# Queries and keys of the first batch entry loaded three rows to a partition and turned by paired products

## The chip, the cores and the metric

One core of one Trainium2 chip runs the whole program. Its engines work side by side, each through its own list of instructions in order: TensorE (PE, with its weight loads shown as PEld), VectorE (DVE), ScalarE (ACT), GpSimd (POOL), and SyncE (SP), which issues the transfers between HBM and on-chip memory. The metric is the device time of one execution in microseconds, the median of several runs.

## What is computed

Attention, then a mixture of eight experts, then a dense layer, all in float32. Two batch entries, eight heads, 576 positions, 64 columns a head:

```python
q_d = q.reshape(B, H, Sd, factor, D).mean(axis=3)      # factor 4, Sd = 144; k_d, v_d alike
out_up = np.repeat(sm_attn(q_d, k_d, v_d), factor, axis=2)
mask = np.abs(pos[:, None] - pos[None, :]) < factor
scores = np.where(mask, scale * q @ k.T, -1e9)
out_local = softmax(scores) @ v
x = (out_up + out_local)                               # then 1152 x 512
...
for e in range(E):
    out += P[:, e:e + 1] * (np.maximum(x @ w1[e], 0.0) @ w2[e])
...
g = softplus(x @ w_in); return g @ w_out
```

So each head has a local part (each position sees those less than four away) and a grouped part (means of four rows attend to means of four rows, and the result is repeated four times).

## The kernel before

The attention runs in eight units of two heads each: units 0 to 3 are batch entry 0, units 4 to 7 entry 1. The stream of work takes the units in order, and of each unit four blocks: "c", the grouped part, and 0, 1, 2, thirds of the 576 positions. For a block, `scores` puts scores into a bank and makes the softmax (maxima on DVE, three exponentials on ACT, sums and scaling on DVE), `turn` transposes the result on PE, and `values` multiplies it with the values. `turn` lags two blocks and `values` three. For units 0 to 3 each `scores` and nearly each `turn` also issues a `stir`, a 128x512 bf16 product of the identity that nobody reads.

Before that, `load_qk` fetches a unit's queries and keys in four transfers (queries and keys, two heads). Partition p holds row 64t + p of the queries (p below 64) or of the keys (64 above), for nine tiles t, the two heads side by side: pieces of 64 floats, 256 B. `setup(g)` is called for three groups of three tiles. It turns each tile with one `nc.tensor.transpose` of 128x128 (L534) into the bank `tb`; DVE adds fours of columns into `qkd` (L539, the grouped queries and keys); ACT scales the keys into `kT` (L550); DVE and ACT copy the two heads' queries into the halves of `fine[g]` (L551, L552), three buffers that all units share. With the third group DVE scales the grouped queries into `flat` (L545). With the first, POOL adds the grouped values `vd` into `vs` (L559, L560).

`load_v` fetches the value windows `vw` (L516, L520; two buffers) and `vd` (L523; one buffer, `bufs=1`, for all units, so that each load waits until POOL has added the one before). Units 0 and 3 take one buffer `qk` for queries and keys; units 1 and 2 borrow places of the first layer's weights, `w1h` and `w1l`, not needed yet.

SP's list is in program order as the scheduler placed it, and a transfer at its head that has to wait holds up all behind it. The expert weights come in through it too (L263, L308); ACT and POOL split them into a high and a low part. From the middle of the attention, pieces of the first expert's products (L866, L954) stand between the attention's products on PE. What is issued where is set by a scheduler, which orders each engine's list by its own estimate; from the second expert on, a planner in the kernel sets it.

Of the kernel before, what the change touches and what calls it, by code (L numbers as in the profile page):

```python
# [9 lines left out]
F32 = mybir.dt.float32  # L10
F32R = mybir.dt.float32r
# [3 lines left out]
ALU = mybir.AluOpType  # L15
AX = mybir.AxisListType
# [4 lines left out]
def attention_moe_mlp(ctx: ExitStack, tc: tile.TileContext, q, k, v, w_gate, w1, w2, w_in, w_out, out):  # L21
    nc = tc.nc
    B, H, S, D = q.shape
    NT, DM = out.shape
    E, _, FF = w1.shape
    F2 = w_out.shape[0]
    P = 128
    R = 4
    SD = S // R
    HC = SD // 2  # L30
    QT = 64
    NQ = S // QT
    NB = 3
    CT = SD // NB
    KW = QT + 2 * R
    KD = DM // P
    SCALE = 1.0 / float(D) ** 0.5
# [19 lines left out]
    wp = ctx.enter_context(tc.tile_pool(name="wp", bufs=3))  # L57
# [4 lines left out]
    rows = [ctx.enter_context(tc.tile_pool(name="rows0", bufs=len(TILES[0])))]  # L62
# [32 lines left out]
    ident = const.tile([P, P], F32, name="ident")  # L95
# [357 lines left out]
    ap = at.__enter__()  # L453
# [18 lines left out]
    fine = [ap.tile([P, NB, 2, QT], F32, bufs=1, name=f"fine{g}") for g in range(NB)]  # L472
# [11 lines left out]
    class Unit:  # L484
# [12 lines left out]
        def load_qk(self):  # L497
            b, h0 = self.b, 2 * self.u
            if self.n in (1, 2):
                qk = wp.tile([P, OPS, 2, P], F32R, tag="w1h" if self.n == 1 else "w1l", name="qkw").bitcast(F32)  # L500
                qk = qk.rearrange("p a k c -> p (a k c)")[:, : NQ * 2 * D]
                qk = qk.rearrange("p (t h d) -> p t h d", t=NQ, h=2)
            else:
                qk = ap.tile([P, NQ, 2, D], F32, tag="qk", bufs=1, name="qk")
            self.qk = qk
            for w, src in enumerate((q, k)):
                for hh in range(2):
                    nc.sync.dma_start(
                        qk[w * QT : (w + 1) * QT, :, hh], src[b, h0 + hh].rearrange("(t p) d -> p t d", p=QT)
                    )  # L510

        def load_v(self):
            b, h0 = self.b, 2 * self.u
            self.vw = vw = ap.tile([KW, NQ, 2, D], F32, tag="vw", name="vw")
            for t, w0 in ((0, 0), (NQ - 1, S - KW)):
                nc.sync.dma_start(vw[:, t], v[b, h0 : h0 + 2, w0 : w0 + KW, :].rearrange("h p d -> p h d"))  # L516
            for hh in range(2):
                src = v[b, h0 + hh, QT - R :, :]
                windows = bass.AP(tensor=src.tensor, offset=src.offset, ap=[[D, KW], [QT * D, NQ - 2], [1, D]])
                nc.sync.dma_start(vw[:, 1 : NQ - 1, hh], windows)  # L520
            self.vd = vd = ap.tile([HC, 2, 2, R, D], F32, tag="vd", bufs=1, name="vd")
            for hh in range(2):
                nc.sync.dma_start(vd[:, :, hh], v[b, h0 + hh].rearrange("(c p r) d -> p c r d", c=2, r=R))  # L523

        def setup(self, g):

            if g == 0:
                self.kT = ap.tile([P, NQ, QT], F32, tag="kT", name="kT")
                self.qkd = ap.tile([P, NQ, 2, QT // R], F32, tag="qkd", name="qkd")
            qkd = self.qkd  # L530
            tb = self.bank("tb", 1)
            tiles = slice(NB * g, NB * g + NB)
            for j in range(NB):
                nc.tensor.transpose(  # L534
                    tb[:, j * P : (j + 1) * P], self.qk[:, NB * g + j].rearrange("p h d -> p (h d)"), ident
                )
            tb = tb[:, : NB * P]
            tbv = tb.rearrange("x (t w p) -> x t w p", t=NB, w=2)
            nc.vector.tensor_reduce(  # L539
                qkd[:, tiles].rearrange("x t w g -> x (t w) g"),  # L540
                tb.rearrange("x (t g r) -> x t g r", g=QT // R, r=R), axis=AX.X, op=ALU.add,
            )
            for hh in range(2 if g == NB - 1 else 0):
                half = slice(hh * D, (hh + 1) * D)
                nc.vector.tensor_scalar(  # L545
                    self.flat[half, :, hh].rearrange("x i (j g) -> x i j g", j=NB),
                    qkd[half, :, 0].rearrange("x (i j) g -> x i j g", i=NB),
                    SCALE / (R * R), None, op0=ALU.mult,
                )
            nc.scalar.mul(self.kT[:, tiles], tbv[:, :, 1], SCALE)  # L550
            nc.vector.tensor_copy(fine[g][:D, :, 0], tbv[:D, :, 0])  # L551
            nc.scalar.copy(fine[g][D:, :, 1], tbv[D:, :, 0])  # L552
            if g:
                return
            vd = self.vd

            self.vs = vs = ap.tile([HC, 2, 2, D], F32, tag="vs", name="vs")
            for c in range(2):
                nc.gpsimd.tensor_tensor(vd[:, c, :, 0:2, :], vd[:, c, :, 0:2, :], vd[:, c, :, 2:4, :], op=ALU.add)  # L559
                nc.gpsimd.tensor_tensor(vs[:, c], vd[:, c, :, 0, :], vd[:, c, :, 1, :], op=ALU.add)  # L560
# [505 lines left out]
    for n in range(len(stream) + LAG + 1):  # L1066
        if n < len(stream):
            x, blk = stream[n]
            i, j = divmod(n, len(blocks))
# [49 lines left out]
    half, short, done = logits()  # L1119
# [46 lines left out]
    with tc.manual_schedule(engines=engines):  # L1166
# [74 lines left out]
```

## Time and profile before

| | |
|---|---|
| median of 3 runs | 1068.11 us (1066.86 to 1068.22) |
| profiled execution | 1065.88 us, span 1064.0 us |
| PE busy | 1044.2 us, 98% of the span |
| DVE, ACT, POOL busy | 692.5, 570.0, 556.1 us |
| DMA packets under 512 B | 36000 of 135799 |
| mean granted TensorE clock | 0.995 |

The span runs from the first to the last instruction of the program; the execution's own time is 1.88 us longer. An engine's busy time is taken from its instructions' records, and those of PE overlap, so the distance from the start of one group to the start of the next tells better what a product costs. A clock of 1.00 is 2.4 GHz, of 0.50 is 1.2 GHz.

### The profile page before, as it was taken

Reading aid. Unit: us, or ns where it says so; the run is one execution under the profiler, and the core shown is the slowest. Engines: PE = TensorE matmul, PEld = TensorE weight load, DVE = VectorE, ACT = ScalarE, POOL = GpSimd, SP = SyncE. Lnnn points to the kernel's source line nnn. Section 1 sums busy time; section 2 is a strip of 40 time slices with the busy share of each in tenths; the row PEclk is TensorE's granted clock in tenths of the full one; section 3 lists DMA queues with packets and bytes.
Section 4 is the critical chain, followed back from the end, with each engine's and each line's share of the span. In section 5 each row is a group of like instructions: output and inputs, shape, how many; then the busy total and the mean of one; then the engine's idle time right before and its main releaser. Section 6 shows DMA issues by size and latency. Waiting matters only on the chain.

```text
span 1064.0 us, 17733 instructions
## 1 busy us (share of the span) xinstructions
PE 1044.2 (98%) x6417; PEld 925.7 (87%) x6417; DVE 692.5 (65%) x1416; ACT 570.0 (54%) x1479; POOL 556.1 (52%) x575
## 2 busy tenths in 40 slices
PE   7989999999999999999999999999999999999998
PEld 5778888898999989898998989899998999888897
DVE  4896666765656566566756665665664677876674
ACT  4887654435444444454444445444544667666664
POOL 3658433487556575555556666664574413222322
PEclk8999999999999999999999999999999999999999
DMA  9463201233333335243333333443334485533752
GB/s 175 131 136 84 85 21 41 61 94 114 95 115 90 99 94 154 80 128 114 117 114 94 101 108 94 118 126 100 119 99 140 147 295 211 217 149 129 262 202 80
DMA packets 135799, 131.22 MB, mean 123 GB/s; under 512 B 36000, under 2 KB 112032, under 8 KB 135712
## 3 DMA queue, kind: packets, MB, share of 16 engines
q1 hardware_dynamic: 135712, 130.10, 39.9%
q8 instruction: 50, 0.82, 0.3%
q14 instruction: 37, 0.30, 0.1%
HBM read 104.64 MB, written 25.43 MB: 122 GB/s over the span
## 4 chain that ended last, share of the span: by engine, by line
PE 83%; DVE 8%; ACT 5%; POOL 2%; DMA 1%; issue 1%; SPq 0%; ACTq 0%
PE yps L954 41%; PE m L866 37%; POOL ab L830 2%; DVE ab L833 1%; ACT one L828 1%; DVE ab L826 1%; PE sc L582 1%; DVE one L824 1%; DVE xl L439 1%; DVE c L885 1%; PE pv L641 1%; DMA raw<-in_moe_w 1%; ACT ab L815 1%; PE tp L619 1%; PE sc L569 1%
## 5 line engine op out<-in xcount | busy, mean ns | idle before, releaser
L866 PE MATMUL m<-xh,w1h 128*128 128x320 f32 (+1 forms) x1120 | 333.8, 298 | 3.5 <-ACT t L878 2.4
L866 PE MATMUL m<-xl,w1h 128*128 128x320 f32 (+1 forms) x1120 | 331.7, 296 | 1.1 <-DVE xl L439 1.1
L866 PE MATMUL m<-xh,w1l 128*128 128x320 f32 (+1 forms) x1120 | 331.6, 296 | 0.0
L866 PEld LDWEIGHTS m<-xh,w1h 128*128 128x128 f32 x1120 | 211.8, 189 | 20.1 <-ACT t L878 4.0
L866 PEld LDWEIGHTS m<-xl,w1h 128*128 128x128 f32 x1120 | 211.9, 189 | 14.4 <-DVE xl L439 1.5
L866 PEld LDWEIGHTS m<-xh,w1l 128*128 128x128 f32 x1120 | 211.8, 189 | 0.3 <-issue 0.2
L954 PE MATMUL yps<-w2h,hh 128*128 128x512 f32 x502 | 198.9, 396 | 0.0
L954 PE MATMUL yps<-w2l,hh 128*128 128x512 f32 x502 | 198.3, 395 | 0.0
L954 PE MATMUL yps<-w2h,hl 128*128 128x512 f32 x502 | 195.9, 390 | 0.0
L954 PE MATMUL yps<-w2h,h 128*128 128x512 f32 x436 | 152.8, 392 | 0.0
L293 POOL TENSOR_TENSOR w1l<-sums,w1h 128x512 fp32r<-128x512 f32 x72 | 99.5, 1394 | 90.9 <-ACT w1h L291 79.3
L885 DVE TENSOR_TENSOR c<-m,t 128x256 f32<-128x256 f32 (+1 forms) x160 | 72.8, 455 | 114.0 <-PE m L866 68.8
L314 POOL TENSOR_TENSOR w2l<-raw,w2h 128x512 fp32r<-128x512 f32 x72 | 98.8, 1391 | 60.0 <-ACT w2h L312 59.8
L803 ACT ACTIVATE hh<-c 128x256 fp32r<-128x256 f32 (+1 forms) x138 | 60.8, 444 | 127.7 <-DVE c L885 127.5
L830 POOL TENSOR_TENSOR ab<-one,ab 128x320 f32<-128x320 f32 (+1 forms) x64 | 55.3, 866 | 141.0 <-ACT one L828 140.9
L984 DVE SCALAR_TENSOR_TENSOR acc<-yps,pr,acc 128x512 f32<-128x512 f32 x117 | 87.2, 745 | 53.0 <-PE yps L954 52.4
L805 DVE SCALAR_TENSOR_TENSOR hl<-c,hh 128x256 fp32r<-128x256 f32 (+1 forms) x138 | 93.3, 679 | 31.7 <-ACT hh L803 30.1
L954 PEld LDWEIGHTS yps<-w2h,hl 128*128 128x128 f32 x502 | 94.4, 188 | 21.6 <-issue 0.2
L954 PEld LDWEIGHTS yps<-w2h,hh 128*128 128x128 f32 x502 | 94.7, 189 | 12.5 <-DVE small L589 0.2
L878 ACT COPY t<-m 128x256 f32<-128x256 f32 (+1 forms) x160 | 62.6, 398 | 77.9 <-PE m L866 77.7
L954 PEld LDWEIGHTS yps<-w2l,hh 128*128 128x128 f32 x502 | 94.8, 189 | 10.7
L954 PEld LDWEIGHTS yps<-w2h,h 128*128 128x128 f32 x436 | 82.1, 188 | 14.7
(141 smaller groups left out, 1647.2 us busy)
## 6 DMA issues: line engine op xcount, KB each, us to landing
raw<-in_moe_w SPq DMA_DIRECT2D x72, 256.0 KB
raw<-in_moe_w SPq DMA_DIRECT2D x36, 512.0 KB
w1h<-s_in SPq DMA_DIRECT2D x14, 896.0 KB
w1l<-s_in SPq DMA_DIRECT2D x14, 896.0 KB
raw<-in_moe_w_in SPq DMA_DIRECT2D x32, 256.0 KB
raw<-in_moe_w_out SPq DMA_DIRECT2D x16, 512.0 KB
w2l<-s_out SPq DMA_DIRECT2D x14, 512.0 KB
w2h<-s_out SPq DMA_DIRECT2D x14, 512.0 KB
```

Source lines behind the costliest of these rows:

```text
L293: behind(chain, nc.gpsimd.tensor_tensor(lo[:, part], sums, hi[:, part].bitcast(F32), op=ALU.subtract))
L314: behind(chain, nc.gpsimd.tensor_tensor(lo[:, i], raw[:, i], hi[:, i].bitcast(F32), op=ALU.subtract))
L439: nc.vector.tensor_tensor(xl[s][:, i, kk], src, xh[s][:, i, kk].bitcast(F32), op=ALU.subtract)
L569: nc.tensor.matmul(sc[:rows, i * w : (i + 1) * w], self.flat[:, i].rearrange("x h q -> x (h q)"), self.qkd[:, :, 1], start=True, stop=True,)
L803: nc.scalar.activation(hh, c, AF.Relu)
L805: nc.vector.scalar_tensor_tensor(out=hl, in0=c, scalar=0.0, in1=hh.bitcast(F32), op0=ALU.max, op1=ALU.subtract)
L830: nc.gpsimd.tensor_tensor(ab, one, ab, op=ALU.subtract)
L866: nc.tensor.matmul(b[:, :h], x[:, i, kk, :], y[s][:, i, kk, :], start=(not more and n == 0), stop=(n == 5), skip_group_check=more,)
L878: nc.scalar.copy(t, b[:, :h])
L885: nc.vector.tensor_tensor(c, b[:, :h], t, op=ALU.add)
L954: nc.tensor.matmul(y, a[:, f, tok], b[:, f, :], start=(start and m == 0), stop=(stop and m == 5))
L984: nc.vector.scalar_tensor_tensor(out=acc[t], in0=y, scalar=pr[:, t, e : e + 1], in1=acc[t], op0=ALU.mult, op1=ALU.add,)
```

## The change

For units 0 to 3, `load_qk` reads the rows as (g p j): partition p of group g holds rows 192g + 3p + j, j from 0 to 2, which lie one behind the other in memory, so a piece is 192 floats, 768 B. In the buffer the head now stands outside of j, and a turned tile would mix heads; so each transpose becomes two products with the identity, one for each head (64 stationary columns), which write 64 partitions of the bank, every third column. The bank then holds queries and keys in the order of the positions. The bank's order is changed for all units (queries ahead of keys); units 4 to 7 keep loads and transposes. The grouped values of units 1 and 2 go into places of the second layer's weights, `w2h` and `w2l`.

```diff
             if self.n in (1, 2):
                 qk = wp.tile([P, OPS, 2, P], F32R, tag="w1h" if self.n == 1 else "w1l", name="qkw").bitcast(F32)
                 qk = qk.rearrange("p a k c -> p (a k c)")[:, : NQ * 2 * D]
+            else:
+                qk = ap.tile([P, NQ * 2 * D], F32, tag="qk", bufs=1, name="qk")
+            self.thirds = self.n < 4
+            if self.thirds:
+                qk = qk.rearrange("p (g h j d) -> p g h j d", g=NB, h=2, j=NB)
+            else:
                 qk = qk.rearrange("p (t h d) -> p t h d", t=NQ, h=2)
-            else:
-                qk = ap.tile([P, NQ, 2, D], F32, tag="qk", bufs=1, name="qk")
...
+                    rows = src[b, h0 + hh]
+                    if self.thirds:
+                        rows = rows.rearrange("(g p j) d -> p g j d", g=NB, j=NB)
+                    else:
+                        rows = rows.rearrange("(t p) d -> p t d", p=QT)
+                    nc.sync.dma_start(qk[w * QT : (w + 1) * QT, :, hh], rows)
...
-            self.vd = vd = ap.tile([HC, 2, 2, R, D], F32, tag="vd", bufs=1, name="vd")
+            if self.n in (1, 2):
+                vd = wp.tile([P, 2, DM], F32R, tag="w2h" if self.n == 1 else "w2l", name="vdw").bitcast(F32)
+                vd = vd[:HC].rearrange("p a (h r d) -> p a h r d", h=2, r=R)
+            else:
+                vd = ap.tile([HC, 2, 2, R, D], F32, tag="vd", bufs=1, name="vd")
...
             for j in range(NB):
-                nc.tensor.transpose(
-                    tb[:, j * P : (j + 1) * P], self.qk[:, NB * g + j].rearrange("p h d -> p (h d)"), ident
-                )
+                if self.thirds:
+                    to = tb.rearrange("x (w p j) -> x w p j", w=2, j=NB)[:, :, :, j]
+                    for hh in range(2):
+                        nc.tensor.matmul(
+                            to[hh * D : (hh + 1) * D], self.qk[:, g, hh, j],
+                            ident.rearrange("k (w p) -> k w p", w=2), start=True, stop=True,
+                        )
+                else:
+                    to = tb.rearrange("x (w t p) -> x w t p", w=2, t=NB)[:, :, j]
+                    nc.tensor.transpose(to, self.qk[:, NB * g + j].rearrange("p h d -> p (h d)"), ident)
```

The scheduler's order shifts with it. DVE near the start, where units 0 and 1 are set up and the first softmax begins (`small` holds the maxima; `fine_147` to `fine_149` are the three groups' queries, `flat_150` and `flat_151` the grouped queries of units 0 and 1), before:

```order
L539 TENSOR_REDUCE qkd<-tb 128x96
L551 COPY fine_149<-tb 64x3x64
L551 COPY fine_147<-tb 64x3x64
L539 TENSOR_REDUCE qkd<-tb 128x96
L551 COPY fine_148<-tb 64x3x64
L589 TENSOR_REDUCE small<-sc 96x3
L589 TENSOR_REDUCE small<-sc 128x3 x2
L539 TENSOR_REDUCE qkd<-tb 128x96
L545 TENSOR_SCALAR flat_151<-qkd 64x3x48 x2
L595 TENSOR_SCALAR small<-sc 96x3
```

and with the change:

```order
L557 TENSOR_REDUCE qkd<-tb 128x96
L568 COPY fine_149<-tb 64x3x64
L568 COPY fine_147<-tb 64x3x64
L557 TENSOR_REDUCE qkd<-tb 128x96
L606 TENSOR_REDUCE small<-sc 96x3
L606 TENSOR_REDUCE small<-sc 128x3 x2
L568 COPY fine_148<-tb 64x3x64
L557 TENSOR_REDUCE qkd<-tb 128x96
L563 TENSOR_SCALAR flat_151<-qkd 64x3x48 x2
L612 TENSOR_SCALAR small<-sc 96x3
```

The three reductions for the maxima moved ahead of the copy into `fine_148`.

PE in the middle of entry 0, where unit 3 is turned (`tb`) beside unit 2's scores (`sc`) and unit 1's values (`pv`), before:

```order
L582 MATMUL sc<-kT,fine_147 128x72 x3
L534 MATMUL tb<-ident,qk 128x128 x6
L630 MATMUL pv<-etc,vs 64x144 x4
L619 MATMUL tp<-ident,ex 72x128 x3
L479 LDWEIGHTS identb
L479 MATMUL sc<-identb 128x512
L576 LDWEIGHTS identb
L576 MATMUL sc<-mask,identb 128x216
L582 MATMUL sc<-kT,fine_148 128x72 x3
```

and with the change:

```order
L586 MATMUL sc<-qkd,flat_150 96x144 x3
L550 MATMUL tb<-ident,qk 64x128 x3
L647 MATMUL pv<-etc,vs 64x144 x4
L636 MATMUL tp<-ident,ex 72x128 x3
L479 LDWEIGHTS identb
L479 MATMUL sc<-identb 128x512
L593 LDWEIGHTS identb
L593 MATMUL sc<-mask,identb 128x216
L599 MATMUL sc<-kT,fine_148 128x72 x3
L550 MATMUL tb<-ident,qk 64x128 x9
```

Of twelve products that stand for six transposes, three stay ahead of the values and the rest went behind the scores of `fine_148`, with three of the next group; the last six of unit 3 stand behind a block's values. Unit 2's eighteen stand as 7, 5 and 6, each group between other work.

SP, from unit 2's queries and keys to the first expert's weights (`raw_584`, `raw_694`) and the value windows, before:

```order
L508 DMA qkw<-in_q 64x9x64 x2
L508 DMA qkw<-in_k 64x9x64 x2
L508 DMA qk<-in_q 64x9x64
L523 DMA vd<-in_v 72x2x256 x2
L508 DMA qk<-in_q 64x9x64
L508 DMA qk<-in_k 64x9x64 x2
L685 DMA wg<-in_moe_w_gate 128x4x8
L263 DMA raw_584<-in_moe_w 128x4x128 x2
L308 DMA raw_694<-in_moe_w 128x2x512
L523 DMA vd<-in_v 72x2x256 x4
L516 DMA vw<-in_v 72x2x64 x2
```

and with the change (`vdw` are the borrowed places):

```order
L535 DMA vdw<-in_v 72x2x256 x2
L517 DMA qkw<-in_q 64x3x192 x2
L517 DMA qkw<-in_k 64x3x192 x2
L535 DMA vdw<-in_v 72x2x256 x2
L517 DMA qk<-in_q 64x3x192 x2
L517 DMA qk<-in_k 64x3x192 x2
L702 DMA wg<-in_moe_w_gate 128x4x8
L535 DMA vd<-in_v 72x2x256 x2
L263 DMA raw_611<-in_moe_w 128x4x128 x2
L308 DMA raw_727<-in_moe_w 128x2x512
L523 DMA vw<-in_v 72x2x64 x2
```

The grouped values of units 1 to 3 moved ahead of the first expert's weights, and only unit 3's still takes the shared buffer.

## Rows read from the trace of the kernel before

**Rows 1.** Windows: stretch, its length, busy PE, PEld, DVE, ACT, POOL, PEclk, DMA share, GB/s

```profile
13.60:16.70 3.10, 0.00 (x0) 0.00 (x0) 2.42 (x10) 2.81 (x19) 1.65 (x4) 0.93 1.36 136
16.70:23.10 6.40, 6.36 (x27) 5.01 (x28) 2.58 (x12) 2.69 (x11) 0.87 (x2) 0.50 1.17 173
23.10:34.40 11.30, 11.30 (x114) 8.95 (x113) 8.20 (x30) 8.67 (x39) 3.59 (x7) 1.00 0.57 145
34.40:46.40 12.00, 12.00 (x126) 9.47 (x125) 10.59 (x32) 11.75 (x51) 9.70 (x13) 1.00 0.51 120
46.40:57.60 11.20, 7.03 (x79) 5.35 (x79) 10.83 (x29) 8.59 (x33) 9.64 (x12) 0.98 0.80 182
57.60:60.70 3.10, 3.07 (x13) 2.72 (x14) 2.87 (x6) 1.56 (x7) 3.10 (x4) 0.51 0.91 198
...
75.00:140.00 65.00, 64.94 (x555) 55.58 (x554) 45.64 (x124) 46.38 (x164) 40.49 (x42) 1.00 0.30 78
```

**Rows 2.** Chain that ended last, 9 to 20 us: start us, us, what

```profile
5.58 4.03 DMA qkw<-in_k
...
12.82 0.62 DVE small L589
```

**Rows 3.** Timeline of PE, 5 to 18 us: start, us, instruction, [idle before <-releaser]

```profile
6.50 1.18 PE L534 MATMUL tb<-ident,qk 128*128 128x128 f32 x9
...
9.74 0.52 PE L534 MATMUL tb<-ident,qkw 128*128 128x128 f32 x3 [1.88 <-DMA qkw<-in_k]
...
11.89 0.90 PE L569 MATMUL sc<-qkd,flat 128*96 128x144 f32 x6
12.62 0.38 PE L479 MATMUL tp<-identb 128*128 128x512 bf16 x1
...
16.74 1.17 PE L609 MATMUL tp<-ident,ex 96*72 96x96 f32 x6 [3.15 <-DVE ex L597]
```

**Rows 4.** Waits of PE, 46.2 to 75 us: in total, times, longest

```profile
PE sc L569 <- ACT et L620: 1.7, 1, 1.7
```

**Rows 5.** DMA queues, 2.3 to 9.7 and 24 to 27 us: packets, MB, share

```profile
q1 hardware_dynamic: 5630, 1.40, 104.4%
...
q1 hardware_dynamic: 1042, 0.93, 104.2%
```

**Rows 6.** Timeline of SP, issues of keys and of grouped values

```profile
4.90 1.32 SPq L508 DMA_DIRECT2D qkw<-in_k  x2
...
8.29 0.91 SPq L523 DMA_DIRECT2D vd<-in_v  x2
```

**Rows 7.** Timeline of PE, 26 to 37 us; an FP32 product has two records

```profile
27.65 0.57 PE L641 MATMUL pv<-et,vw 72*64 72x64 f32 x12
28.15 0.44 PE L609 MATMUL tp<-ident,ex 96*72 96x96 f32 x3
...
29.85 0.49 PE L534 MATMUL tb<-ident,qkw 128*128 128x128 f32 x3
30.27 0.57 PE L641 MATMUL pv<-et,vw 72*64 72x64 f32 x12
...
34.44 0.82 PE L534 MATMUL tb<-ident,qk 128*128 128x128 f32 x6
35.18 0.72 PE L630 MATMUL pv<-etc,vs 72*64 72x144 f32 x8
35.83 0.52 PE L619 MATMUL tp<-ident,ex 128*72 128x128 f32 x3
```

**Rows 8.** Timeline of DVE, near 11 and near 46 us

```profile
10.30 0.56 DVE L539 TENSOR_REDUCE qkd<-tb 128x96 f32<-128x384 f32 x1 [0.71 <-PE tb L534]
...
12.46 0.35 DVE L551 COPY fine<-tb 64x192 f32<-64x192 f32 x1 [0.40 <-ACT kT L550]
...
46.46 0.38 DVE L589 TENSOR_REDUCE small<-sc 128x3 f32<-128x216 f32 x1 [0.89 <-PE sc L582]
```

**Rows 9.** SP's waits, 0 to 80 us: in total, times, longest

```profile
SPq L523 <- POOL vs L560: 7.6, 4, 2.7
```

More of the change, by code (lines that the diff above doesn't have):

```diff
@@ L507, in load_qk @@
                 for hh in range(2):
-                    nc.sync.dma_start(
-                        qk[w * QT : (w + 1) * QT, :, hh], src[b, h0 + hh].rearrange("(t p) d -> p t d", p=QT)
-                    )
+                    rows = src[b, h0 + hh]
[4 more added lines that the diff above has]
+                    nc.sync.dma_start(qk[w * QT : (w + 1) * QT, :, hh], rows)
         def load_v(self):
@@ L520, in load_v @@
                 nc.sync.dma_start(vw[:, 1 : NQ - 1, hh], windows)
-            self.vd = vd = ap.tile([HC, 2, 2, R, D], F32, tag="vd", bufs=1, name="vd")
+            if self.n in (1, 2):
[3 more added lines that the diff above has]
+                vd = ap.tile([HC, 2, 2, R, D], F32, tag="vd", bufs=1, name="vd")
+            self.vd = vd
             for hh in range(2):
@@ L528, in setup @@
                 self.kT = ap.tile([P, NQ, QT], F32, tag="kT", name="kT")
-                self.qkd = ap.tile([P, NQ, 2, QT // R], F32, tag="qkd", name="qkd")
+                self.qkd = ap.tile([P, NB, 2, CT], F32, tag="qkd", name="qkd")
             qkd = self.qkd
@@ L532, in setup @@
             tiles = slice(NB * g, NB * g + NB)
+            tb = tb[:, : NB * P]
             for j in range(NB):
-                nc.tensor.transpose(
-                    tb[:, j * P : (j + 1) * P], self.qk[:, NB * g + j].rearrange("p h d -> p (h d)"), ident
-                )
-            tb = tb[:, : NB * P]
-            tbv = tb.rearrange("x (t w p) -> x t w p", t=NB, w=2)
+                if self.thirds:
[8 more added lines that the diff above has]
+                    nc.tensor.transpose(to, self.qk[:, NB * g + j].rearrange("p h d -> p (h d)"), ident)
             nc.vector.tensor_reduce(
-                qkd[:, tiles].rearrange("x t w g -> x (t w) g"),
-                tb.rearrange("x (t g r) -> x t g r", g=QT // R, r=R), axis=AX.X, op=ALU.add,
+                qkd[:, g].rearrange("x w g -> x (w g)"),
+                tb.rearrange("x (g r) -> x g r", r=R), axis=AX.X, op=ALU.add,
             )
@@ L545, in setup @@
                 nc.vector.tensor_scalar(
-                    self.flat[half, :, hh].rearrange("x i (j g) -> x i j g", j=NB),
-                    qkd[half, :, 0].rearrange("x (i j) g -> x i j g", i=NB),
-                    SCALE / (R * R), None, op0=ALU.mult,
-                )
-            nc.scalar.mul(self.kT[:, tiles], tbv[:, :, 1], SCALE)
-            nc.vector.tensor_copy(fine[g][:D, :, 0], tbv[:D, :, 0])
-            nc.scalar.copy(fine[g][D:, :, 1], tbv[D:, :, 0])
+                    self.flat[half, :, hh], qkd[half, :, 0], SCALE / (R * R), None, op0=ALU.mult,
+                )
+            tbv = tb.rearrange("x (w t p) -> x w t p", w=2, p=QT)
+            nc.scalar.mul(self.kT[:, tiles], tbv[:, 1], SCALE)
+            nc.vector.tensor_copy(fine[g][:D, :, 0], tbv[:D, 0])
+            nc.scalar.copy(fine[g][D:, :, 1], tbv[D:, 0])
             if g:
```

## The prediction

> **What bounds the kernel now.** I read the page's stretches first, then the chain of waits, then the engines' rows around each edit. After 75 us TensorE (PE) is busy for 64.94 of 65.00 us, with DVE, ACT and POOL at 46, 46 and 40 [rows 1]: whatever time the first stage gains or loses reaches the end unchanged. So only the first 75 us have to be costed, and they fall into four pieces. **Entry, 0 to 16.7:** the chain runs from the landing of unit 1's keys at 9.61 (5.58 + 4.03) through DVE and ACT to the scores' maxima at 12.82 [rows 2], from which the softmax follows. PE turns unit 0 at 6.50, stands 1.88 us until unit 1 has landed, and stands 3.15 us more for the first softmax, until 16.74 [rows 3]. **16.7 to 23.1:** PE works without a break at a granted clock of 0.50, which is 1.2 GHz, after 13.6 to 16.7 in which it did nothing [rows 1]. **23.1 to 46.4:** PE is busy for 11.30 of 11.30 and 12.00 of 12.00 us at 2.4 GHz [rows 1]. The reader is to see that PE alone is the bound here: its busy time covers both stretches whole, while DVE has 4.5 us free and ACT 2.9. **46.4 to 75:** DVE is the bound (10.83 of 11.20 us), PE is busy for 7.03 of 11.20 [rows 1], and its longest wait, 1.7 us, ends on ACT [rows 4].
>
> **The transfers.** Queries and keys of units 0 to 3 now move in 768 B pieces instead of 256 B, 768 packets a unit for 2304. From 2.3 to 9.7 us 5630 packets of 1.40 MB kept 16 engines full (104.4%) for 7.4 us: 16 x 7.4 x 1.044 / 5630 = 22 ns each. From 24 to 27 us 1042 packets of 0.93 MB took 16 x 3 x 1.042 / 1042 = 48 ns each at a mean of some 900 B [rows 5]. By size 768 B lies near 40 ns, so a unit's queries and keys cost 768 x 40 / 16 = 1.9 us instead of 2304 x 22 / 16 = 3.2. The pair of issues to SP takes 1.32 us for 576 small pieces each and 0.91 for 144 of 1 KB each [rows 6]; 192 pieces lie between. Unit 1 then lands between 6.5 us (issues as cheap as those of 1 KB) and 8.3 (issues as now, 1.3 us saved in the packets), instead of 9.61. Nothing else before 46 us waits for a transfer on PE, so the transfers' gain is this one wait.
>
> **The turning.** Nine transposes of a unit become 18 FP32 products with 64 stationary and 128 moving columns. Transposes: three at 29.85 take until 30.27, six at 34.44 until 35.18, and a 64-wide group follows both; 0.42 = 3a + s and 0.74 = 6a + s give a = 0.107 us and s = 0.10, the cost of going over to 64-wide work [rows 7]. The trace has no 64-wide product of 128 moving columns, but two neighbours: six of 64 columns from 27.65 to 28.15, four of 144 from 35.18 to 35.83 [rows 7]. 0.50 = 384c + f and 0.65 = 576c + f give c = 0.00078 us a column and f = 0.20 a group. One product of 128 columns is 0.10 us, and a group of its own pays 0.20 + 0.10 = 0.30 on top. This I take, since both neighbours have the same stationary width. The upper bound is the product with 96 stationary columns: three of 144 columns took 11.89 to 12.62, 0.24 each, or 0.22 for 128 columns [rows 3]; the stride of three elements with which the new products write has no row either, and is taken into that bound. The lower bound, two products of a pair at once, would be 0.05; the six of 64 columns already alternate the two heads and show no such gain. The Trainium skill, TensorEngine Tiling, Tiling Modes, says that a change of tiling mode drains TensorE. The trace agrees with 0.10 on the way in; by that rule the change pays at each separate group, as in the sum here.
>
> In 23.1 to 46.4 PE turns units 2 and 3. Unit 2: groups of 7, 5 and 6, each with other work on both sides: 18 x 0.10 + 3 x 0.30 = 2.70, for 9 x 0.107 = 0.96 before: +1.74. Unit 3: three and six stand directly beside 64-wide products that pay the change-over in any case, nine stand alone: 1.80 + 0.30 = 2.10 for 0.96: +1.14. **Together +2.9 us, all on the path**, since nothing hides PE there. At 0.22 a product it is +7.2, at 0.05 it is +1.1.
>
> **The entry, step by step.** Unit 0: products from 6.50, one change-over, 18 x 0.10: until 8.5 instead of 7.5. DVE's three reductions (0.5 each) now wait for six products each, the third ends near 9.25; two copies and two scalings (1.2) follow, so DVE turns to unit 1 at about 10.2, against 10.30 now after a wait of 0.71 for PE [rows 8]. The 1.88 us that PE waited are gone, yet DVE is next late and keeps all but 0.1. Then the order helps: the maxima of unit 0's grouped block stand ahead of a copy that waited 0.40 for ACT [rows 8], and start when their scores are there, near 12.15 instead of 12.82. Unit 1's last group (six products and 0.30, so 0.9 for 0.33) sends DVE's reduction and scalings, which precede the softmax's next step, some 0.3 later. PE gets its transposes at 16.3 instead of 16.74: **-0.4**, between -0.7 (that last group hidden) and +0.5 (the reordering eaten by it). At 1.2 GHz the lead is kept as time on the softmax's chain, not doubled.
>
> **The grouped values.** Units 1 and 2 no longer share one buffer with unit 0. SP stood 7.6 us, four times, for POOL to free it [rows 9]. What is queued behind it there are weights and windows; none of them is waited for by PE before 46 us, so this gives nothing there. POOL's order moves: one weight subtraction (1.0 us) goes behind a sum of grouped values that waits for its load, and a sum (0.86) goes behind the next weights, which cancels to within 0.2; the next expert's weights are issued ahead of a unit's grouped values instead of behind them. In 46.4 to 75 DVE starts from a wait for PE's scores (0.89 at 46.46 [rows 8]), so PE's delay goes through it. ACT's short wait for those weights and part of the collisions with POOL may fall away: **-0.5**, between -2.5 (nearly all of the delay lost in PE's waits there, as that of [rows 4]) and +0.8. The borrowed weight places are free again long before the third pair of weights takes them: nothing.
>
> **Sum.** -0.4 + 2.9 - 0.5 = +2.0 us. The profiled execution took 1065.88 us, 1.88 over its span of 1064.0; with the change 1067.9. The median of the three runs, 1068.11, lies 2.2 above that execution, so I add the same 2.0 there: 1070.1. A comparison of this kernel can tell about 0.2%, 2.1 us; the sum lies just inside.
>
> **Rivals.** *The clock.* 1.2 GHz held from about 16.3 (0.93 over 13.6 to 16.7 leaves 0.4 us at half) to 23.1 the first time, but only from 57.6 to 60.7 the second [rows 1]. With PE busier before 13.6 and from 16.3 on, the first could be as short as the second, or not come. 3.3 us of work would then take half, but the softmax of unit 0's third block (3.9 us from maxima to transposes, as 12.82 to 16.74) lets through about 1.0: 1069.1. The Trainium skill, TensorE: Matmul & The Clock Gate, Part 4, says that transposes do not count as PE-busy the way products do; by it the products would hold the clock up and this rival would come true. For it speaks that work from 57.6 brought the clock back sooner; against it, that PE still stands 2.5 us before 16.3. *Swallowed.* DVE and ACT could have enough slack after 46.4 that the +2.9 dissolves in PE's waits there: 1068.1 or so. Against it: DVE waits for PE at 46.46. *Dear products.* If 64-wide products cost what those with 96 stationary columns do, or the strided writes slow them, 0.22 each: +4.3 more in the dense stretch and some 0.8 in the entry, 1075; it decides against the change from about 0.11 us a product. The Trainium skill, TensorE: Matmul & The Clock Gate, Terms, calls the transpose mode 4 times faster for FP32; by that a product would be 4 x 0.107 = 0.43, and the sum about +14; the 64-wide rows speak against it. *All at once.* The clock held, the softmax a further 0.7 earlier and the delay swallowed: -0.4 - 0.7 - 1.0 + 0 = -2.1 and more, 1065.8; it needs all of them.
>
> **How the numbers follow.** Forecast 0.50 (own range 1068.8 to 1071.4), clock 0.18, swallowed 0.12, dear products 0.12, all at once 0.08. Slower by over 0.2%: nearly half of the forecast lies over 1070.25, 0.24, and all of dear products, 0.12: 0.36. Faster: 0.08. The rest, 0.56, within. The range leaves out dear products and all at once, 0.20 together: 1067.0 to 1073.0, from the clock and the swallowing at their best to products of 0.13 us.
>
> **What would show it.** After: unit 1 landed by 8.3, PE's first softmax transposes near 16.3; groups of 64x128 products at 0.10 each and 0.9 per six; PE still without a wait from 23 to 46, and the last score group before 46.4 about 2.5 us later than now; after 75 us the same rows as before, shifted by the sum. I am wrong if the products take 0.2, if PE's low clock moves or vanishes, or if PE's waits between 46 and 75 shrink by as much as it came late.

## The result and the profile after

The changed kernel took 1073.09 us (median of seven runs, 1071.13 to 1077.69) against 1067.24 for the kernel before, a ratio of 1.0057 (95% interval 1.0042 to 1.0072): 5.9 us slower, where 2.0 were forecast and 1073.0 was the range's upper end. A second series (`e5_changed_again` below) gave 1.0050 (1.0034 to 1.0066). The profiled execution took 1073.81 us, its span is 1071.7, 7.7 over that of before.

The stretches of [rows 1] after the change (length, busy PE, PEld, DVE, ACT, POOL, PEclk, DMA share, GB/s):

```profile
13.60:16.70 3.10, 1.83 (x17) 0.89 (x16) 2.47 (x9) 2.77 (x17) 0.85 (x3) 1.00 1.01 184
16.70:23.10 6.40, 5.72 (x33) 4.50 (x34) 2.91 (x12) 3.15 (x14) 3.09 (x6) 0.73 1.01 172
23.10:34.40 11.30, 11.30 (x128) 8.53 (x125) 7.88 (x30) 8.69 (x37) 2.77 (x5) 1.00 0.46 120
34.40:46.40 12.00, 12.00 (x137) 9.47 (x137) 8.96 (x28) 9.03 (x40) 6.16 (x9) 1.00 0.33 83
46.40:57.60 11.20, 10.02 (x95) 8.22 (x94) 9.78 (x30) 9.05 (x40) 8.20 (x9) 0.85 0.66 175
57.60:60.70 3.10, 1.10 (x12) 0.70 (x11) 3.10 (x6) 3.08 (x10) 2.94 (x6) 1.00 0.73 164
60.70:75.00 14.30, 9.31 (x81) 7.93 (x81) 12.03 (x25) 7.00 (x34) 8.93 (x10) 0.76 0.37 85
75.00:140.00 65.00, 63.24 (x565) 54.56 (x564) 47.10 (x135) 46.77 (x174) 37.53 (x40) 1.00 0.37 96
```

From 23.1 to 46.4 it is as forecast: PE is busy throughout. The new hole is at 57.6 to 75: PE busy for 10.4 of 17.4 us, against 15.4 before. PE there (start, us, instruction, idle before and its releaser):

```profile
48.54 0.80 PE L599 MATMUL sc<-kT,fine 128*128 128x72 f32 x6
...
57.98 0.72 PE L647 MATMUL pv<-etc,vs 72*64 72x144 f32 x8
65.56 1.73 PE L586 MATMUL sc<-qkd,flat 128*96 128x144 f32 x6 [6.86 <-DVE flat L563]
67.08 0.63 PE L479 MATMUL tp<-identb 128*128 128x512 bf16 x1
```

PE stands 6.86 us for `flat`, the scaled grouped queries of unit 4; before, the same scores began at 57.63. DVE works all that time, at one pair of scalings:

```profile
58.65 0.89 DVE L439 TENSOR_TENSOR xl<-xf,xh 128x256 fp32r<-128x256 f32 x1
59.46 5.95 DVE L563 TENSOR_SCALAR flat<-qkd 64x144 f32<-64x144 f32 x2
65.44 0.18 DVE L613 RECIPROCAL small<-small 128x3 f32<-128x3 f32 x1
```

and POOL, meanwhile, passes from one instruction to the next without a pause:

```profile
59.22 1.05 POOL L577 TENSOR_TENSOR vs<-vd 72x128 f32<-72x128 f32 x2
60.23 1.26 POOL L276 TENSOR_TENSOR w1l<-raw,w1h 128x512 fp32r<-128x512 f32 x1
61.45 1.26 POOL L314 TENSOR_TENSOR w2l<-raw,w2h 128x512 fp32r<-128x512 f32 x1
62.67 0.72 POOL L242 TENSOR_TENSOR sums<-raw 128x256 f32<-128x256 f32 x1
63.35 1.26 POOL L314 TENSOR_TENSOR w2l<-raw,w2h 128x512 fp32r<-128x512 f32 x1
64.57 0.72 POOL L242 TENSOR_TENSOR sums<-raw 128x256 f32<-128x256 f32 x1
```

All 16 scalings, before and after (count, shortest/median/longest in ns, first and last start):

```profile
L545 DVE TENSOR_SCALAR flat<-qkd x16: 282/297/300, 9.0 to 110.9; 64x144 f32<-64x144 f32 x16
```

```profile
L563 DVE TENSOR_SCALAR flat<-qkd x16: 241/256/3360, 10.5 to 117.7; 64x144 f32<-64x144 f32 x16
```

The layout of the grouped sums is what makes this pair slow, as the experiments below show. Before, a scaling read 9 runs of 16 elements and wrote 3 runs of 48; now it reads 3 runs of 48 and writes 3 runs of 48. That form is 40 ns faster where POOL stands (0.24 to 0.26 us), and takes up to 3.36 us where POOL works: of the eight scalings that met a POOL instruction, seven took 0.37 us or more and one 0.24. The diff shows the new layout; the prediction took the scalings over at their old price.

### The profile page after: what moved, and what is told of

Read it like the earlier page. It is cut to its first block, busy times and chain, and to the rows that moved or that the text cites. A ratio compares the mean times of both kernels' runs of the same rounds, so it can differ in the third digit from the quotient of the medians.

```text
span 1071.7 us, 17945 instructions
## 1 busy us (share of the span) xinstructions
PE 1051.4 (98%) x6525; PEld 931.4 (87%) x6525; DVE 695.9 (65%) x1416; ACT 569.9 (53%) x1479; POOL 555.2 (52%) x575
## 4 chain that ended last, share of the span: by engine, by line
PE 83%; DVE 10%; ACT 4%; POOL 2%; issue 1%; ACTq 0%; DVEq 0%; POOLq 0%
PE yps L971 40%; PE m L883 36%; POOL ab L847 2%; DVE ab L850 1%; ACT one L845 1%; PE sc L599 1%; DVE ab L843 1%; DVE xl L439 1%; DVE one L841 1%; DVE flat L563 1%; PE tb L550 1%; DVE c L902 1%; PE tp L636 1%; PE sc L586 1%; PE pv L658 1%
## 5 line engine op out<-in xcount | busy, mean ns | idle before, releaser
L293 POOL TENSOR_TENSOR w1l<-sums,w1h 128x512 fp32r<-128x512 f32 x72 | 98.6, 1381 | 94.9 <-ACT w1h L291 82.2
```

The lines of the kernel that those rows point to most:

```text
L293: behind(chain, nc.gpsimd.tensor_tensor(lo[:, part], sums, hi[:, part].bitcast(F32), op=ALU.subtract))
```

## The experiments

"One run" below means the changed kernel with the grouped queries in one run of 144, so that the scaling reads 1 run and writes 3:

```diff
-                self.qkd = ap.tile([P, NB, 2, CT], F32, tag="qkd", name="qkd")
+                self.qkd = ap.tile([P, 2, NB, CT], F32, tag="qkd", name="qkd")
...
-                qkd[:, g].rearrange("x w g -> x (w g)"),
-                tb.rearrange("x (g r) -> x g r", r=R), axis=AX.X, op=ALU.add,
+                qkd[:, :, g],
+                tb.rearrange("x (w g r) -> x w g r", w=2, r=R), axis=AX.X, op=ALU.add,
...
-                    self.flat[half, :, hh], qkd[half, :, 0], SCALE / (R * R), None, op0=ALU.mult,
+                    self.flat[half, :, hh], qkd[half, 0], SCALE / (R * R), None, op0=ALU.mult,
...
-                        self.qkd[:, :, 1], start=True, stop=True,
+                        self.qkd[:, 1], start=True, stop=True,
```

In the table "3 to 3" is a scaling that reads 3 runs and writes 3; each ratio is to the kernel before, measured beside the run.

| run | scaling | units turned by products | median us | ratio to before, 95% interval |
|---|---|---|---|---|
| e1_single_port | one run | 0 to 3 | 1072.08 | 1.0042 (1.0025 to 1.0059) |
| e2_shared_values | 3 to 3 | 0 to 3, values in one buffer | 1071.02 | 1.0038 (1.0023 to 1.0052) |
| e3_before_like_runs | 3 to 3 | none, kernel before | 1074.93 | 1.0071 (1.0048 to 1.0094) |
| e4_two_units | one run | 0, 1 | 1066.01 | 0.9985 (0.9970 to 1.0000) |
| e5_changed_again | 3 to 3 | 0 to 3 | 1073.86 | 1.0050 (1.0034 to 1.0066) |
| e6_units_2_3 | one run | 2, 3 | 1074.13 | 1.0066 (1.0048 to 1.0085) |
| e7_no_products | one run | none | 1066.01 | 0.9986 (0.9973 to 0.9998) |
| e8_unit_1 | one run | 1 | 1064.69 | 0.9977 (0.9965 to 0.9989) |
| e9_more_stirs | one run | none, 12 stirs more | 1070.18 | 1.0025 (1.0009 to 1.0041) |
| e10_unit_1_like_runs | 3 to 3 | 1 | 1071.01 | 1.0031 (1.0017 to 1.0045) |
| e11_fewer_stirs | one run | 0 to 3, 12 stirs fewer | 1072.42 | 1.0051 (1.0031 to 1.0071) |
| e12_unit_1_fewer_stirs | one run | 1, 12 stirs fewer | 1068.99 | 1.0012 (1.0001 to 1.0024) |
| e13_like_unit_4 | 3 to 3 in unit 4 alone | none | 1067.96 | 1.0016 (1.0002 to 1.0030) |
| e14_like_five | 3 to 3 in units 1, 2, 4, 6, 7 | none | 1068.79 | 1.0020 (1.0008 to 1.0032) |
| e15_stirs_6 | one run | none, 6 stirs more | 1068.17 | 1.0019 (1.0007 to 1.0030) |
| e16_stirs_15 | one run | none, 15 stirs more | 1069.75 | 1.0037 (1.0023 to 1.0051) |
| e17_one_stir_unit_3 | one run | none, 1 stir more | 1065.85 | 0.9987 (0.9971 to 1.0004) |
| e18_one_stir_unit_2 | one run | none, 1 stir more | 1067.43 | 1.0001 (0.9990 to 1.0013) |

### The form of the scaling

**The changed kernel with one run.**

> The changed kernel, with only the layout of the grouped sums altered: the grouped queries of a unit lie as one run of 144 in their buffer, so that the scaling into flat reads 1 run of 144 and writes 3 runs of 48, where the changed kernel reads and writes 3 runs of 48. Theory A (the scaling, in the form of 3 runs to 3 runs, cannot run while POOL runs; with unlike runs it does not care): all 16 scalings take 0.28 to 0.30 us beside POOL too, as in the kernel before; the one of unit 4 that took 3.36 + 2.57 us takes 0.6, PE's wait of 6.86 us before unit 4's grouped scores shrinks to under 2.5, and the time is 1070 us (1068.5 to 1071.5), the delay that PE had brought along from the dense stretch. Theory B (the scaling is slow because POOL's list became denser there, whatever its form): it stays at 3 to 6 us and the time at 1073 (1072 to 1074.5). Theory C (the 5.9 us come mostly from the products and the clock): PE's wait stays above 4 us with another releaser, 1072 to 1073.

All 16 scalings took 279 to 300 ns, though POOL worked beside four of the pairs; PE came to unit 4's grouped scores at 60.17 us without a wait. The mechanism of theory A holds, its size doesn't: the time fell by only 1 to 2 us (the intervals overlap), to where theory C had it, so most of the loss has another source. The scheduler, too, answered with another order, so this pair alone doesn't price the form.

**The changed kernel with the shared buffer, and once more.** The first puts back the one line `self.vd = vd = ap.tile([HC, 2, 2, R, D], F32, tag="vd", bufs=1, name="vd")`; the second is unedited.

> The changed kernel, but all units' grouped values go through the one buffer again; PE, DVE and ACT keep the changed kernel's order row for row, only SP's and POOL's lists differ near the first expert's weights. Theory A (form of the scaling against POOL): at least one pair of scalings beside a run of POOL instructions still takes over 2 us; 1073 us (1071 to 1075). Theory B (the borrowed places, by moving POOL's and SP's lists, made the stall): all scalings under 0.5 us and 1068 to 1070. Theory C (products and clock): 1072 to 1074 with the same low stretches of the granted clock.

> The changed kernel itself once more, beside the next three on one chip, for its scaling and its clock in a second profile. Theory A (port): wherever POOL runs beside one of the 16 scalings it takes 0.4 us or more, and 0.26 or less where POOL stands, but how long unit 4's pair takes differs from one execution to the next (1.4 us in the kernel with the shared values, 5.9 in the first profile), so the median stays at 1072 to 1074 and the runs scatter over 3 us or more. Theory B (a fixed order of POOL and DVE): unit 4's pair takes 5.9 us again within 0.5.

In the repeat, unit 4's pair took 3360 and 2572 ns again, and PE waited 6.86 us again: no lottery, POOL and DVE meet there in the same way in both profiles, and my theory A of that run was wrong. With the shared buffer, POOL's sums stand elsewhere in its list and the pair took 0.77 + 0.67 us, PE's longest wait there was 1.7 us. Neither theory A of that run (a pair over 2 us) nor theory B (all under 0.5) came true: the longest pair, unit 3's, took 0.92 + 0.80 us. The borrowed places thus decided how long the stall was, the form that there was one. The times lie too close for more (1.0038 against 1.0050).

**The kernel before with 3 to 3, and unit 1 alone with 3 to 3.** Only the layout of the sums differs from the kernel before, or from `e8_unit_1` (below).

```diff
-                self.qkd = ap.tile([P, NQ, 2, QT // R], F32, tag="qkd", name="qkd")
+                self.qkd = ap.tile([P, NB, 2, CT], F32, tag="qkd", name="qkd")
```

> The kernel before, with nothing but the changed kernel's layout of the grouped sums (3 x 2 x 48), so that the scaling reads and writes 3 runs of 48; transposes, loads and grouped values as before. Theory A: each scaling takes 0.24 to 0.26 us where POOL stands and 0.4 to 3.4 us where POOL runs (12 of 16 fell beside POOL before); the time grows by what the longest one adds on PE's path, 0 to 6 us, most likely +2: 1069 (1067.5 to 1073). Theories B and C: all scalings at 0.30 or less, 1067 to 1068.

> The kernel with unit 1 alone turned by products, but with the changed kernel's layout of the grouped sums, so that the scaling reads and writes 3 runs of 48 again. If the form of the scaling costs time wherever POOL is busy beside it: scalings at 0.4 us and more there, and 1064.7 plus what it cost so far (1.4 between the changed kernel and the one with the single run, 7.5 between the kernel before and the one with like runs): 1068 (1066 to 1072). If it only struck by chance in those orders: 1064 to 1066, with no pair over 1 us.

Both lost clearly: 7.5 us over the kernel before, and 5.4 over `e8_unit_1` (3.2 over before, which lies 2.2 above `e8_unit_1`). Scalings beside POOL took 0.4 to 1.3 us in the one, 0.3 to 2.0 in the other, save one of about 0.25 in each. But the order had shifted in both, and in the profile of `e3_before_like_runs` PE's waits ahead of grouped scores come to only 1.5 us, so the 7.5 are not shown to be the form's. Two more runs kept the order.

**The same order, the form alone.** A condition chooses the layout by unit; with unit 4, or 1, 2, 4, 6 and 7, the scheduler keeps the order of `e7_no_products` on every engine, row for row.

```diff
+                self.like = self.n == 4
+                if self.like:
+                    qkd = ap.tile([P, NB, 2, CT], F32, tag="qkd", name="qkd")
+                    qkd = qkd.rearrange("p i w g -> p w i g")
+                else:
+                    qkd = ap.tile([P, 2, NB, CT], F32, tag="qkd", name="qkd")
```

> The kernel without products (1066.0), where only unit 4's grouped sums lie as in the changed kernel, so that its scaling alone reads and writes 3 runs of 48; every engine keeps the order of the kernel without products, row for row. Port: unit 4's pair, which met POOL without a pause there (54.7 to 60 us) and took 0.6, now takes 1.5 to 6 us, PE's wait before unit 4's grouped scores grows from 1.7 by the excess over 0.6, and the time to 1068.5 (1067 to 1072). Order alone (the kernels with this form were slower because the scheduler shifted their lists): 1066 (1065 to 1067), the pair at 0.5.

> The same with the like runs in units 1, 2, 4, 6 and 7; still the order of the kernel without products on every engine. Port: each of these scalings that has POOL beside it takes 0.4 us or more; the time is that of the kernel with unit 4 alone, or up to 2 us over it where units 2 and 6 lie on PE's path: 1069 (1067 to 1074). Order alone: 1066 (1065 to 1067).

DVE and PE without the form (`e7_no_products`):

```profile
54.90 0.60 DVE L563 TENSOR_SCALAR flat<-qkd 64x144 f32<-64x144 f32 x2
```

```profile
55.65 1.73 PE L586 MATMUL sc<-qkd,flat 128*96 128x144 f32 x6 [1.69 <-ACT fine L569]
```

and with it in unit 4 alone (`e13_like_unit_4`):

```profile
53.48 4.72 DVE L569 TENSOR_SCALAR flat<-qkd 64x144 f32<-64x144 f32 x2
```

```profile
58.35 1.72 PE L592 MATMUL sc<-qkd,flat 128*96 128x144 f32 x6 [5.81 <-DVE flat L569]
```

In one pair of eight 0.60 becomes 4.72 us, PE's wait 1.7 becomes 5.8, and the ratios' intervals, 0.9973 to 0.9998 and 1.0002 to 1.0030, don't meet: +2 to +3 us. Five units cost little more than unit 4 (its pair took 2.13 + 2.58 there, PE again waited 5.8). **Shown:** the form costs this, at one place, with nothing else moved.

### The products

**No products, units 0 and 1, unit 1, units 2 and 3.** All with one run; the only further edit is the condition.

```diff
-            self.thirds = self.n < 4
+            self.thirds = self.n == 1
```

> As the first of these kernels, but only units 0 and 1 are loaded three rows to a partition and turned by products; units 2 and 3 keep the old loads and transposes. If the products of units 2 and 3 cost what the trace of the changed kernel shows in PE's dense stretch (PE went from 0.7 us ahead at 24 us to 2.8 behind at 44), the time is 2.9 us (2 to 3.5) under that of the first kernel, about 1067. If PE's delay there is swallowed later, both are the same within 0.7.

> The changed kernel with the grouped queries in one run (scaling at 0.28 to 0.30), and products only for units 2 and 3; units 0 and 1 keep the old loads and transposes. If the products of these two units are what the first kernel with all four lost, 1070.5 us (1069.5 to 1072), about 4 over the kernel with units 0 and 1 alone. If only all four together cost so much (the entry shifts what the rest meets), 1068 (1067 to 1069).

> No products at all: old loads and transposes for all units, the changed order of the bank, the grouped queries in one run, and the borrowed places for the values of units 1 and 2. PE, DVE and ACT have the order of the kernel before, row for row; only POOL's sums and SP's issues of the values move. If the borrowed places neither help nor hurt: 1067.4 within 1.0. If they make POOL run without a pause at a worse moment: 1069 to 1071.

> As the kernel without products, but unit 1 alone is loaded three rows to a partition and turned by products; the order on PE, DVE and ACT is that of the kernel before. If the faster landing of unit 1 is worth what the entry's working said, unit 1's turning starts near 8 us instead of 9.74, PE's first softmax transposes near 16.0 to 16.4 instead of 16.74, and the time is 0.3 to 1.0 us under the kernel without products. If DVE's chain holds the entry anyway, they come within 0.2 of 16.74 and both kernels take the same time.

Products for units 2 and 3 cost 6.1 us (0 and 1, against all four) and 8.1 (none, against 2 and 3), twice what was expected; in units 0 and 1 they cost nothing. The borrowed places and the bank's order, with PE, DVE and ACT in the order of before, gained a little at most (0.9973 to 0.9998). Unit 1 alone has the lowest ratio and is faster than the kernel before and the changed kernel; its interval overlaps those of no products and of units 0 and 1. PE's entry in it, and without products:

```profile
8.47 1.35 PE L550 MATMUL tb<-ident,qkw 128*64 128x128 f32 x12 [0.21 <-DMA qkw<-in_k]
...
16.66 0.69 PE L626 MATMUL tp<-ident,ex 96*72 96x96 f32 x6 [2.09 <-DVE ex L614]
```

```profile
9.90 0.52 PE L556 MATMUL tb<-ident,qkw 128*128 128x128 f32 x3 [1.80 <-DMA vw<-in_v]
...
16.89 0.98 PE L626 MATMUL tp<-ident,ex 96*72 96x96 f32 x6 [3.15 <-DVE ex L614]
```

Unit 1 is turned 1.4 us sooner, but the first softmax transposes come only 0.23 us sooner, within 0.2 of 16.74: DVE's chain holds the entry, as the second expectation had it. The times, 1.3 us apart, don't tell (the intervals overlap).

**PE's time by itself.** Stirs are work of 0.215 us that nobody waits for. Twelve more in the groups of transposes of units 2 and 3:

```diff
+            stir(tb, 2 if self.n in (2, 3) else 0)
```

> The kernel without products, with two stirs ahead of each of the six groups of transposes of units 2 and 3: 12 x 0.215 = 2.6 us of dummy work more on PE between 23 and 52 us, about as much as the products of these units add, with nothing else of the change. If time on PE in that stretch is on the path one to one: 1066.0 + 2.6 = 1068.6 (1067.5 to 1070). If what the products of units 2 and 3 cost (6 to 8 us between the kernels with and without them) comes with any delay of that size: 1072 (1070.5 to 1074). If it belongs to the products or to the order that they bring: 1066 to 1067.

Six more ahead of unit 1's turns, then fifteen (6 in place of 3 below), these two in one order on all engines but for two neighbours on ACT that changed places:

```diff
-                stir(tp, 1 if self.n < 4 else 0)
+                stir(tp, 3 if self.n == 1 else 1 if self.n < 4 else 0)
```

> The kernel without products, with two more stirs ahead of each of unit 1's three turns: 6 x 0.215 = 1.3 us more of PE between 24 and 34 us; the scheduler's order shifts with it. It is the base of the next kernel. If PE's time alone counts: 1067.3 (1066.3 to 1068.3); if a shifted order costs by itself: 1069 or more.

> Five more stirs ahead of each of these three turns, 9 more than the last kernel and otherwise in the same order on every engine: 9 x 0.215 = 1.9 us more of PE. If PE's time in the dense stretch is on the path one to one: 1.9 us (1.0 to 2.8) over the last kernel. If it is swallowed in the waits after 46 us: within 0.7. If it multiplies by what follows (clock, DVE beside POOL): over 3.

Twelve fewer in units 2 and 3:

```diff
-            stir(sc, 1 if self.n < 4 else 0)
+            stir(sc, 1 if self.n < 2 else 0)
...
-                    stir(tp, 1 if self.n == 0 or self.n < 4 and c == 0 else 0)
+                    stir(tp, 1 if self.n == 0 or self.n in (1, 3) and c == 0 else 0)
...
-                stir(tp, 1 if self.n < 4 else 0)
+                stir(tp, 1 if self.n in (0, 1, 3) else 0)
```

> Products for all four units and the grouped queries in one run, as in the first kernel (1072.1), but without the stirs of unit 2 and those of unit 3's scores: 12 x 0.215 = 2.6 us of PE's time less between 23 and 50 us. If PE's time there is on the path one to one: 1069.5 (1068.5 to 1070.5); if the delay is paid twice, as the products' was: 1066 to 1067.5; if it is not PE's time that the products cost: 1072 (1071 to 1073).

> The kernel with unit 1 alone turned by products (1064.7), without the same 12 stirs. If PE's time in the dense stretch is on the path: 1062 (1061 to 1063). If DVE is the bound behind it, as the windows after 46 us say of the kernel before, PE only waits longer there: 1064 to 1065.5, with DVE's rows where they were. If the granted clock falls without the stirs: over 1066.

Between the two kernels of one order, 1.9 us more of PE cost 1.6 us (1.9 by the ratios). That fits one to one, but the intervals overlap, and the two profiles don't bear it out: the second kernel is 1.74 us later at unit 3's grouped scores (46.42 against 44.68) and 0.47 earlier at unit 7's (118.88 against 119.35). Against no products, the six stirs cost 2.6 us (3.5 by the ratios) for 1.3 of work and the twelve of `e9_more_stirs` 3 to 4 us for 2.6, but in both the order shifted as well. The other way it doesn't work: with twelve fewer, PE was busy for 21.3 and 21.1 of the 23.3 us from 23.1 to 46.4 and then waited for DVE, and in `e12_unit_1_fewer_stirs` its clock was at 1.2 GHz from 48.9 to 59.2 and from 66.0 to 76.2. Taking PE's work away gained nothing: `e11_fewer_stirs` took the 1072 us of its third expectation (not PE's time), and `e12_unit_1_fewer_stirs` lost 3 to 4 us, as its last one (the clock) had it.

**A shifted order by itself.** One stir more, ahead of the turning of unit 3's or unit 2's grouped block.

```diff
-                    stir(tp, 1 if self.n == 0 or self.n < 4 and c == 0 else 0)
+                    stir(tp, 2 if self.n == 3 and c == 0 else 1 if self.n == 0 or self.n < 4 and c == 0 else 0)
```

> The kernel without products (1066.0) with one single stir more, 0.2 us of PE, ahead of the turning of unit 3's grouped block. The scheduler answers with another order behind it (the rest of units 3 to 7 stands differently on PE, DVE and ACT). If a shifted order costs by itself: 1068 to 1070. If it does not: 1066.2 (1065.2 to 1067.2), and the cost of the products beyond their own time needs another cause.

> The same single stir ahead of the turning of unit 2's grouped block, which shifts the order from there on, over half as many rows again. A shifted order costs by itself: 1068 to 1071. It does not: 1066.2 (1065.2 to 1067.2).

The order shifted over hundreds of rows; the first cost nothing, the second 1.1 us (1.6 by the ratios), with an interval that overlaps that of no products. So a shifted order need not cost the 3 to 5 us that the products cost beyond their own time; that the order they bring does is not excluded.

**Where that rest shows.** With products but without the slow form, PE does not wait at unit 4's grouped scores and loses its time after them. Start of the grouped scores on PE, us:

| | unit 4 | unit 5 | unit 6 | unit 7 |
|---|---|---|---|---|
| before | 57.63 | 74.01 | 93.31 | 115.21 |
| changed | 65.56 | 81.10 | 100.55 | 122.00 |
| e1_single_port | 60.17 | 77.50 | 98.56 | 121.43 |
| e6_units_2_3 | 59.08 | 80.33 | 103.06 | 125.23 |
| e7_no_products | 55.65 | 74.73 | 94.04 | 115.75 |

In the profiles with products in units 2 and 3, unit 5's grouped values are fetched at 51.5 to 52.9 us, against 47.07 in the kernel before and 45.20 without products. They are late with more stirs too (52.47 in `e9_more_stirs`, 51.88 in `e16_stirs_15`), so this doesn't belong to the products alone. SP, then POOL (products in 2 and 3, `e6_units_2_3`):

```profile
51.56 0.82 SPq L535 DMA_DIRECT2D vd<-in_v  x2
```

```profile
57.70 1.57 POOL L576 TENSOR_TENSOR vd<-vd 72x256 f32<-72x256 f32 x2 [5.24 <-DMA vd<-in_v]
```

and without products (`e7_no_products`):

```profile
45.20 0.74 SPq L535 DMA_DIRECT2D vd<-in_v  x2
```

```profile
48.51 1.41 POOL L576 TENSOR_TENSOR vd<-vd 72x256 f32<-72x256 f32 x2 [0.19 <-DMA vd<-in_v]
```

POOL stands, then does its work in one piece beside DVE, which is the bound there. 60 to 75 us, products in 2 and 3, then none:

```profile
60.00:75.00 15.00, 11.25 (x85) 9.40 (x84) 14.13 (x36) 10.89 (x43) 14.43 (x14) 0.78 0.54 135
```

```profile
60.00:75.00 15.00, 14.07 (x106) 11.89 (x106) 11.15 (x38) 10.94 (x47) 6.29 (x8) 0.72 0.38 103
```

The six kernels with POOL busy for over 12 us in this stretch (e1, e2, e6, e9, e11, e16) are all at ratios of 1.0025 and more; those under 10 without the slow form lie at 0.9977 to 1.0019. So the kernels with much late work on POOL are slow ones. But no run moved it alone, and in `e18_one_stir_unit_2` POOL stood 3.91 us for the same load at a ratio of 1.0001: the cause stays open.

## Why the prediction was wrong

**The entry, forecast -0.4:** wrong. Unit 0's turning took until 9.51 instead of 8.5, so unit 1, for which PE no longer waited, was turned at 9.79, against 9.74 in [rows 3], and the softmax transposes came at 17.38, not 16.3:

```profile
6.74 2.83 PE L550 MATMUL tb<-ident,qk 128*64 128x128 f32 x36
...
9.79 0.88 PE L550 MATMUL tb<-ident,qkw 128*64 128x128 f32 x12
...
17.38 0.82 PE L626 MATMUL tp<-ident,ex 96*72 96x96 f32 x6 [1.21 <-DVE ex L614]
```

The step that failed is 18 x 0.10 from 6.50. Of the 1.0 us too little, 0.24 is a later start (6.74) and an estimated 0.4 the clock: PE's rose at 7.55 in this profile, at 6.02 in that of before, and the products ran at 1.2 GHz until then. +0.64 at the softmax transposes; by 24 us PE was 0.7 ahead all the same, since the clock was low for 3.4 us instead of 6.8.

**The turning of units 2 and 3, forecast +2.9:** right in kind, a little small. A product takes 0.109 us, a group its change-over. PE went from 0.66 us ahead at 24 us to 2.92 behind at the score group of 48.54 (45.62 before): +3.6, without a wait. The forecast was 2.5 behind there.

**The stage from 46.4 to 75, forecast -0.5 between -2.5 and +0.8:** this is the step that failed, in two terms. The rows say about +5: PE 2.9 behind at 48.5, 7.9 behind at unit 4's scores (65.56 against 57.63). I costed the collisions of DVE and POOL as something that could only fall away, and took the scalings at 0.3 each, though the diff changes their operands. I also read PE's wait of 1.7 us in [rows 4] as one for ACT, which the view names. The rows of DVE and PE say otherwise:

```profile
56.88 0.60 DVE L545 TENSOR_SCALAR flat<-qkd 64x144 f32<-64x144 f32 x2
57.63 1.73 PE L569 MATMUL sc<-qkd,flat 128*96 128x144 f32 x6 [1.69 <-ACT et L620]
```

PE starts 0.146 us after the pair of scalings has ended, and so it does, to 2 ns, in the changed kernel, `e7_no_products` and `e13_like_unit_4`. Unit 4's pair was on PE's path before the change. The kernel before also had rows that price the form. This scaling reads and writes one like run, first with POOL idle, then beside POOL's L293 (others: 0.68 and 1.01):

```profile
171.90 0.17 DVE L756 TENSOR_SCALAR gcs<-gcs 128x8 f32<-128x8 f32 x1
179.94 1.07 DVE L756 TENSOR_SCALAR gcs<-gcs 128x8 f32<-128x8 f32 x1
```

while `flat` took 0.28 to 0.30 with POOL beside most of the sixteen. The Trainium skill has the rule, in VectorE: DVE Perf Modes, Mode 2×_2P: an operation with one source uses both read ports if the outermost dimensions of source and destination, in SBUF, are even, or odd and equal (3 and 3 are, 9 and 3 or 144 and 3 are not); and the Trainium skill says in SBUF — State Buffer, Who interferes with whom, that such an instruction contends with GpSimd for a port pair that one holds for a whole instruction. The traces agree: 3 to 3 waits for POOL (all but one of eight in the changed kernel), 9 to 3 and 144 to 3 don't. They add that DVE stood through four POOL instructions in a row.

The second term is the moves in POOL's list, which I took to cancel to within 0.2. A weight subtraction went behind a sum, and a sum behind the next weights; but it is the last sum of a unit that frees the buffer, and both moves put it off. Unit 4's came 5.2 us later, and with it the fetch of unit 5's values, for which POOL then stood 3.00 us instead of 0.31. Before:

```profile
46.19 0.86 POOL L560 TENSOR_TENSOR vs<-vd 72x128 f32<-72x128 f32 x2
47.07 0.74 SPq L523 DMA_DIRECT2D vd<-in_v  x2
50.50 1.41 POOL L559 TENSOR_TENSOR vd<-vd 72x256 f32<-72x256 f32 x2 [0.31 <-DMA vd<-in_v]
```

and with the change:

```profile
51.38 0.86 POOL L577 TENSOR_TENSOR vs<-vd 72x128 f32<-72x128 f32 x2
52.27 0.77 SPq L535 DMA_DIRECT2D vd<-in_v  x2
56.47 1.91 POOL L576 TENSOR_TENSOR vd<-vd 72x256 f32<-72x256 f32 x2 [3.00 <-DMA vd<-in_v]
```

What this costs by itself no run shows. What the runs show is that the products of units 2 and 3 cost 6 to 8 us with all that they bring, not 2.9.

**Why not more, then?** The form (+2 to +3 in one place, same order) and the products (+6 to +8) don't add up to 5.9. The table above shows where: with the form PE is 7.9 us late at unit 4's grouped scores and 7.2 at unit 6's; without it, in `e6_units_2_3`, 1.45 and 9.75. What the stall takes is not lost a second time behind it. Why not stays open.

**The rivals.** *Clock:* the first low stretch was shorter, but without products it was too (17.1 to 20.6 in `e7_no_products`), so the products didn't do it, and two more low stretches came with PE's waits (51.9 to 55.3 and 62.2 to 69.0). They don't explain the loss: `e7_no_products` had a longer one, 54.7 to 68.3, and lost nothing. *Swallowed:* not here, the loss grew; whether PE's time by itself would be, the stirs leave open. *Dear products:* right about the size of the loss, wrong about its cause: 0.109, not 0.22; the strided writes cost 0.01 a product at most, against the 0.10 worked out from rows without them. *After 75 us:* not quite as said. The rows of the changed kernel come 6 to 9 us later, 7.7 at the end, but PE was busy for 63.24 of the 65.00 us from 75 to 140, and in `e6_units_2_3` it lost 3.4 more between the grouped scores of units 5 and 6.

## What to carry to other kernels

When a change gives an instruction other access patterns, cost that instruction anew, beside each engine it can meet, even if its element count is the same. Look in the trace of before for any row of the same form with the neighbour busy and idle. When a view names what a wait ended on, check which instruction ended just before it, at the same distance each time. And price work that moves in an engine's list by what it delays elsewhere too (here the release of a buffer, and with it a load), not only by its own length.

## What the hardware showed that was not expected

DVE's 3-to-3 scaling did not get its turn at the boundary between two POOL instructions: in the changed kernel and its repeat it stood through four, which followed each other without a pause, both times for 3360 ns, and in `e13_like_unit_4` through five, for 4207 ns. Subtractions with two SBUF inputs (L439), 0.41 us alone, do likewise: two took 5.26 in `e3_before_like_runs`.

The moment at which PE's clock first rises to 2.4 GHz lay between 5.0 and 8.0 us in the 20 profiles, and the low stretch after it lasted 6.8, 3.4 or, once, 0 us, also among kernels with the same rows up to there. In `e7_no_products`, executions with a mean granted clock of 0.997 took 1063.4 to 1064.0 us and those with 0.990 took 1066.5 to 1068.4. This is more than the 2.0 us that were forecast.
